# A written-out order for a gated recurrence and its MLP: all words re-ordered, h's casts spread over three engines, the verdicts summed in a row

## The chip, the cores and the metric

The kernel runs on one core of a Trainium2 chip. The metric is device time in microseconds (us) of one execution, the median over the runs shown; lower is better. The engines are TensorE (PE in the rows; PEld is its weight load), VectorE (DVE), ScalarE (ACT), GpSimd (POOL) and SyncE (SP), which here issues nearly all DMA transfers. Each engine works through its own queue in order, and an instruction waits at the head of its queue until what it reads is written and what it overwrites is free.

## What is computed

Inputs q, k, v and alpha have 4 batches, 8 heads, 768 time steps and 48 channels. Each head runs a gated recurrence, and the result goes through a gated MLP of 384 to 1536 to 384 on 3072 tokens:

```python
for t in range(S):
    state = alpha[:, :, t, :, None] * state + np.einsum('bhd,bhe->bhde', k[:, :, t], v[:, :, t])
    y[:, :, t] = np.einsum('bhd,bhde->bhe', q[:, :, t], state)
...
g = x @ w_gate
silu = g * (1.0 / (1.0 + np.exp(-g)))
val = x @ w_val
return (silu * val @ w_out).astype(np.float32)
```

The weights and inputs arrive as the reference has them, the weights in 64 bits.

## The kernel before

**Units.** Time is cut into 16 units (4 per batch, 192 steps of three chunks of 64). A unit u is loaded (words La, Lk, Lq, V), its alpha, k and q are turned so that channels lie on partitions (by TensorE for units 0 to 3: the words p, T, ea, ek, cq; by VectorE's 32x32 transposes for the others: tr, tk, tq, line 399), and VectorE runs two scans over them: G backward (line 472), f forward (lines 478 to 482). The word mk puts k into the first scan's result, q multiplies q by the second's, and qc copies its odd heads. K and kc (units 0 to 3) or kr (line 540, the other units) lay k out in rows. TensorE then forms scores (S, line 565), which VectorE masks (ma, line 606), carries the state over the chunks (C, or the carry at line 584; ad and de bring it into V) and forms outputs (Y, lines 658 to 680). From unit 4 on one word Z, a burst (line 682), holds the outputs of unit u - 1, the scores of unit u and its carry.

**From units to blocks.** The outputs are split into a high and a low part in a 32-bit format that TensorE takes in one pass (yh on ScalarE, line 705; yl on VectorE, line 709) and are regrouped to x, 384 tokens by 384 channels, in blocks of two units: with TensorE and copies for units 0 and 1 (R, line 731, and x, line 735), with SP's transfers for the others (xr, line 745).

**Steps.** The MLP of 8 blocks by 12 slices of 128 hidden channels gives 96 steps s: g (gate product, line 760), sl (SiLU to h, ScalarE, line 768), v (value product, line 760), h (h times v, VectorE, line 772), hh (h cast to the one-pass format, line 776), hl (the rest h - hh, line 781), o (out product, line 793). Each of g, v and o is nine matmuls of 384 columns, as hi and lo parts are multiplied hi by hi, hi by lo and lo by hi. The g and v products have one PSUM bank each (gps, vps), and h, hh and hl have two buffers each, so a step holds up the next one when its h is late. Bursts borrow these banks too (the digits behind @ are banks). Finished rows are copied out (ot, line 805) and stored (os, line 819; those listed in HALVED, line 785, in two halves). The first two blocks run in two halves of the hidden channels, with partial sums spilled to DRAM and added again (pl, line 801).

**Weights.** Twenty groups wl0 to wl19, the first three of one slice piece, the others of two, are loaded and cut from 64 bits to 32 in three steps w.v0, w.v1, w.v2 (lines 163 to 178; if v0 is on ScalarE the other two take another form on VectorE), then split into a high part (w.a, line 343) and a low part (w.p, line 347). Group 3 holds v1 and o0, group 7 holds g4 and v4.

**Checks and the verdict.** Weights and alpha are loaded a second time and checked for range by ScalarE (wr and wc, Lc and ck). VectorE folds the results to one number per partition (fl, line 830), TensorE adds the 128 numbers with a matmul against ones (cp, `counted`, line 841), VectorE converts the sum to an integer flag (fg, line 970), and every engine reads it at the end to decide on a fallback (line 1133).

**The order.** Nothing decides the order at run time. The string ORDER (from line 44) is a list of words `engine:name`, with t, v, s, g, y for TensorE, VectorE, ScalarE, GpSimd and SP; the loop at line 978 issues them one by one, so the words of one letter, read in sequence, are that engine's queue:

```python
for word in ORDER.split():
    e, name = word.split(":")
    name, *banks = name.split("@")
    todo.pop(name)(engines[e], *(BANKS[int(x)] for x in "".join(banks)))
```

## Time and profile before

| | us |
|---|---|
| runs (three) | 548.59, 548.66, 551.18 |
| median | 548.66 |
| profiled execution: its own time | 549.81 |
| profiled execution: its span | 548.1 |
| TensorE busy in the span | 528.0 |
| VectorE busy in the span | 400.5 |

The span runs from the first to the last instruction of the profiled execution; its own time has the launch around it. Busy time counts instructions at work, not waits, register work or DMA issues. An engine's row can have a wait in square brackets, in us, and what ended it. In the rows, `x9` counts instructions that are merged into one row, and a duration in a merged row is that of the whole group.

### The profile page before, as it was taken

The numbers are of one execution on the slowest core, as the hardware profiler recorded it, in microseconds if no ns is written. First come the engines' busy times: TensorE is split into PE (matmuls) and PEld (weight loads), VectorE is DVE, ScalarE is ACT, GpSimd is POOL, SyncE is SP. The second block draws the span as 40 slices with busy tenths as digits, with TensorE's granted clock in tenths as the row PEclk, the third lists the DMA queues.
The fourth block names the chain that finished last, engine by engine and source line by source line (L and its number), as shares of the span: only waits on it lengthen the run. The fifth ranks groups of instructions, "written<-read, shape, count | busy, mean of one in ns | idle before, by whom it ended". The sixth has DMA issues, their size and how long they took to land.

```text
span 548.1 us, 13557 instructions
## 1 busy us (share of the span) xinstructions
PE 528.0 (96%) x5350; PEld 513.7 (94%) x5350; DVE 400.5 (73%) x755; ACT 249.4 (45%) x578; POOL 151.2 (28%) x149
## 2 busy tenths in 40 slices
...
GB/s 243 256 263 292 146 173 249 107 139 174 85 187 151 141 106 185 157 120 73 169 76 101 203 158 112 76 136 129 184 153 73 90 50 158 135 58 104 155 50 47
...
## 3 DMA queue, kind: packets, MB, share of 16 engines
...
## 4 chain that ended last, share of the span: by engine, by line
PE 66%; DVE 3%; DMA 2%; SPq 1%; issue 1%; ACT 0%; POOL 0%; DVEq 0%; POOLq 0%
PE v L760 20%; PE ops L793 20%; PE g L760 20%; PE c L680 2%; PE s L565 1%; DMA L<-in_q_dram 1%; PE c L584 1%; PE y L658 1%; PE y L659 1%; DMA xT<-X 1%; SPq L745 1%; DMA V<-in_v_dram 1%; DVE h L772 0%; DVE V L629 0%; DVE K L540 0%
## 5 line engine op out<-in xcount | busy, mean ns | idle before, releaser
L760 PE MATMUL v<-xT,w 128*128 128x384 f32 x864 | 167.3, 337 | 0.6 <-DMA xT<-X 0.6
L760 PE MATMUL g<-xT,w 128*128 128x384 f32 x864 | 166.6, 336 | 0.6 <-ACT h L768 0.4
L793 PE MATMUL ops<-w,hh 128*128 128x384 f32 x576 | 158.5, 336 | 0.0
L760 PEld LDWEIGHTS v<-xT,w 128*128 128x128 f32 x864 | 150.5, 188 | 2.2 <-issue 0.9
L760 PEld LDWEIGHTS g<-xT,w 128*128 128x128 f32 x864 | 150.7, 188 | 1.8 <-ACT h L768 0.9
L781 POOL TENSOR_TENSOR hl<-h,hh 128x384 fp32r<-128x384 f32 x65 | 69.8, 1075 | 285.5 <-ACT hh L776 271.8
L772 DVE TENSOR_TENSOR h<-h,v 128x384 f32<-128x384 f32 x96 | 53.0, 552 | 89.9 <-PE v L760 61.6
L793 PEld LDWEIGHTS ops<-w,hh 128*128 128x128 f32 x576 | 105.5, 188 | 0.3
L768 ACT ACTIVATE h<-g 128x384 f32<-128x384 f32 x96 | 47.1, 490 | 119.6 <-PE g L760 101.0
L776 ACT CAST hh<-h 128x384 fp32r<-128x384 f32 x96 | 49.1, 511 | 112.0 <-DVE h L772 77.4
L793 PE MATMUL ops<-w,hl 128*128 128x384 f32 x288 | 96.8, 336 | 0.0
L540 DVE STREAM_TRANSPOSE K<-Gs 32x192 f32<-32x192 f32 x192 | 71.1, 370 | 3.3
L793 PEld LDWEIGHTS ops<-w,hl 128*128 128x128 f32 x288 | 54.0, 188 | 0.0
L347 POOL TENSOR_TENSOR w<-t,w 128x768 fp32r<-128x768 f32 (+1 forms) x15 | 27.5, 1842 | 34.4 <-ACT w L343 25.3
L781 DVE TENSOR_TENSOR hl<-h,hh 128x384 fp32r<-128x384 f32 x31 | 18.4, 594 | 22.8 <-ACT hh L776 22.7
L481 DVE TENSOR_TENSOR_SCAN AT<-AT,back 128x771 f32<-128x771 f32 x16 | 29.2, 1824 | 0.6
L606 DVE TENSOR_TENSOR X<-s,mask 64x384 f32<-64x384 f32 (+1 forms) x48 | 26.3, 551 | 3.8 <-PE s L565 3.1
L472 DVE TENSOR_TENSOR_SCAN Gs<-AT,inj 128x772 f32<-128x772 f32 x16 | 28.5, 1780 | 0.5 <-ACT AT L866 0.3
L497 POOL TENSOR_TENSOR X<-trq,AT 112x768 f32<-112x768 f32 x11 | 18.7, 1703 | 32.1 <-DMA xT<-X 11.0
L320 ACT ACTIVATE wc<-wc,wbias 128x384 f32<-128x384 f32 x36 | 23.3, 648 | 1.2
...
L893 POOL TENSOR_TENSOR Gs<-trk,Gs 128x768 f32<-128x768 f32 x9 | 15.3, 1700 | 26.0 <-DVE Gs L472 22.2
...
## 6 DMA issues: line engine op xcount, KB each, us to landing
...
```

Source lines behind the costliest of these rows:

```text
L320: nc.scalar.activation(dev, dev, AF.Relu, bias=wbias, scale=-1.0, accum_out=wviol[:, 0, i : i + 1])
L347: eng.tensor_tensor(out=lo, in0=src, in1=hi.bitcast(F32), op=ALU.subtract)
L472: nc.vector.tensor_tensor_scan(*(x.rearrange("p g t -> p (g t)")[:, ::-1] for x in (Gs, AT, inj)), 0.0, op0=ALU.mult, op1=ALU.add)
L481: nc.vector.tensor_tensor_scan(Af, Af, back[:, 1 : n + 1], back[:, 0:1], op0=ALU.mult, op1=ALU.add)
L540: nc.vector.transpose(out=bass.AP(k0.tensor, k0.offset, [k0.ap[0], (G * 2 * D, NU), (2 * D, GF), (1, 32)]), in_=Kg[j * BO + x : j * BO + x ...
L606: nc.vector.tensor_tensor(out=X[r, z, f * GF : (f + 1) * GF, :].rearrange("r g (c t) -> r g c t", c=NU), in0=sps[f][r].rearrange("r g (c t ...
L760: nc.tensor.matmul(pt, wsp[kind, f][a][:, kt * P : (kt + 1) * P], xT[blk][:, b_, kt, :], start=(n == 0), stop=(n == 3 * KT - 1),)
L768: nc.scalar.activation(h, acc.pop(("g", blk, f)), AF.Silu)
L772: nc.vector.tensor_tensor(out=h, in0=h, in1=acc.pop(("v", blk, f)), op=ALU.mult)
L776: nc.scalar.copy(out=hh, in_=acc["h", blk, f])
L781: eng.tensor_tensor(out=hl, in0=acc.pop(("h", blk, f)), in1=hh.bitcast(F32), op=ALU.subtract)
L793: nc.tensor.matmul(ops[blk][i], h[b_][:, i * P : (i + 1) * P], wsp["o", f][a], start=(first and n == 0), stop=(last and n == 2),)
```

## The change

The order is another one throughout: all five queues are dealt anew. It holds the same words but for two (cp goes, vr comes), and 113 words stand under another engine's letter, among them 44 of the 96 hh, all of which were ScalarE's: 22 now stand under VectorE and 22 under GpSimd. Of hl 18 move from GpSimd to VectorE and 13 the other way; the remaining 38 are cuts and splits of the weights, copies (qc, ot, pa, pq, vc, x) and products (mk, q) that change between VectorE, ScalarE and GpSimd. In place of the matmul against ones, the word vr sends the 128 numbers by a transfer of SP into one row of the identity matrix's tile, and VectorE sums that row and converts the sum. One store is no longer halved.

The code:

```diff
-    def hidden_hi(blk, f):
+    def hidden_hi(blk, f, eng):
         hh = acc["hh", blk, f] = p2.tile([P, NB], F32R, tag="hh", name=f"hh{blk}_{f}", bufs=NH)
-        nc.scalar.copy(out=hh, in_=acc["h", blk, f])
+        (eng.copy if eng is nc.scalar else eng.tensor_copy)(out=hh, in_=acc["h", blk, f])
...
-    HALVED = ((6, 0), (6, 1), (6, 2))
+    HALVED = ((6, 0), (6, 1))
...
-    ones = cp.tile([P, 1], F32, name="ones")
...
-        nc.vector.memset(ones, 1.0)
...
-    def counted(bank):
-        oks.append(ps.tile([1, 1], F32, tag=bank, name="cps"))
-        nc.tensor.matmul(oks[-1], ones, oks[-2], start=True, stop=True)
+    row = ident[0:1, 0:P]
+
+    def verdict_row(eng):
+        eng.dma_start(out=row.rearrange("o (p x) -> o p x", x=1), in_=oks[-1])
+
+    def counted():
+        total = cp.tile([1, 1], F32, name="total")
+        nc.vector.tensor_reduce(total, row, axis=AX.X, op=ALU.add)
+        nc.vector.tensor_copy(out=flag, in_=total)
...
-    todo["cp"] = lambda eng, bank: counted(bank)
-    todo["fg"] = lambda eng: eng.tensor_copy(out=flag, in_=oks[-1])
+    todo["vr"] = lambda eng: verdict_row(eng)
+    todo["fg"] = lambda eng: counted()
```

The order, old (-) and new (+), up to the first products:

```diff
-s:first y:La0 s:pa0 t:Ta0@23 s:ea0 y:wl0 y:Lq0 s:pq0 v:w0v0 v:w0v1 v:w0v2 v:G0 v:f0 t:Tq0@03 v:q0 y:La1 s:pa1 t:Ta1@72
-s:w0a v:w0p y:Lk1 s:pk1 y:Lk0 s:pk0 y:wl1 s:w1v0 t:Tk1@14 y:Lq1 t:Tk0@05 g:pq1 y:V0.2 y:V0.3 y:V0.1 v:w1v1 v:mk0 s:ea1
-v:G1 s:ek1 v:mk1 s:qc0 t:K0.2@0 s:kc0.2 t:K0.1@7 s:kc0.1 t:K0.0@2 s:kc0.0 t:S0@05 t:Tq1@71 s:cq1 v:f1 g:q1 g:qc1
-y:V0.4 y:wl3 y:V0.0 y:V0.5 t:C0.0@2 s:ad0.0 t:K1.1@4 t:K1.0@1 t:C0.1@7 y:wl2 y:V1.1 y:V1.4 y:La2 s:w3v0 s:ad0.1
-s:kc1.0 v:ma0.1 v:ma0.0 v:ma0.2 v:w2v0 v:pa2 v:w2v1 v:w1v2 v:w3v1 s:vc0 t:C0.2@2 s:ad0.2 t:K1.2@7 s:kc1.2 s:kc1.1
-t:Y0@36 s:yh0.0 y:La3 t:Ta2@20 s:pa3 s:ea2 y:Lk2 y:V1.0 s:w1a s:yh0.1 g:w1p y:Lq2 y:V1.3 y:V1.5 y:V1.2 v:w3v2 v:de1
-t:S1@71 t:C1.0@2 s:ad1.0 v:yl0.0 v:ma1.2 t:Ta3@15 t:C1.1@4 s:ad1.1 t:C1.2@0 y:wl4 s:w4v0 s:ad1.2 g:pq2 g:pk2 g:vc1
-v:ma1.1 v:yl0.1 v:ma1.0 t:Y1@64 s:yh1.0 v:w2v2 v:w2a s:yh1.1 t:R0.1@0 t:R0.2@3 t:Tq2@72 s:x0.2 s:x0.1 s:cq2 v:G2
-v:yl1.0 v:yl1.1 t:R1.1@6 s:x1.1 v:w4v1 v:w4v2 t:Tk2@74 v:mk2 v:f2 v:q2 y:Lk3 s:pk3 t:R1.0@0 t:R0.0@6 y:V2.4 s:x0.0
-s:x1.0 t:R1.2@7 s:x1.2 t:K2.0@2 s:kc2.0 g:w2p y:wl5 s:w5v0 y:V2.2 y:V2.0 y:Lq3 g:pq3 s:w4a t:Tk3@34 t:K2.1@7 s:kc2.1
-t:g0 s:sl0 y:V3.1 y:V2.1 y:wl7 y:V2.3 y:V2.5 v:de2 g:vc2 g:lm0 y:V3.2 y:wl8 y:wl6 y:V3.3 y:V3.0 v:w5v1 s:ea3 v:G3
...
+s:first y:La0 s:pa0 t:Ta0@23 s:ea0 y:wl0 y:Lq0 s:pq0 t:Tq0@03 v:w0v0 v:w0v1 v:w0v2 v:G0 v:f0 v:q0 s:w0a v:w0p y:La1
+s:pa1 t:Ta1@15 y:Lk1 s:pk1 y:Lk0 s:pk0 y:wl1 s:w1v0 t:Tk1@26 v:w1v1 t:Tk0@47 v:mk0 s:ea1 s:ek1 v:G1 y:wl2 s:w2v0 v:mk1
+y:Lq1 s:pq1 y:V1.4 t:K0.2@6 t:K0.0@2 t:K0.1@1 s:kc0.2 y:V0.4 s:kc0.0 s:kc0.1 v:w1v2 y:V0.2 y:V0.0 y:V0.1 t:S0@43
+t:Tq1@27 s:cq1 v:f1 g:q1 g:qc1 y:wl3 v:w3v0 v:ma0.2 y:V0.3 y:V0.5 t:C0.0@0 s:ad0.0 t:K1.0@6 s:kc1.0 v:qc0 v:ma0.1
+t:C0.1@5 s:ad0.1 v:ma0.0 t:K1.1@7 s:kc1.1 y:La2 y:V1.0 t:C0.2@6 s:vc0 s:ad0.2 t:K1.2@2 s:kc1.2 s:w1a s:pa2 t:S1@07
+t:Y0@16 s:yh0.0 y:V1.1 y:V1.5 y:wl4 y:V1.3 y:V1.2 v:de1 t:C1.0@3 v:w2v1 v:w2v2 v:w3v1 v:w3v2 s:ad1.0 t:Ta2@45 s:ea2
+s:yh0.1 t:C1.1@3 s:ad1.1 s:w3a y:Lq2 y:La3 v:ma1.2 t:C1.2@5 v:ma1.0 v:ma1.1 g:vc1 t:Y1@24 v:yl0.1 v:yl0.0 s:ad1.2
+s:pa3 t:R0.2@6 t:R0.1@7 t:Ta3@53 g:pq2 y:V2.3 y:V2.4 y:Lk2 y:Lk3 y:V2.5 g:w1p g:pk2 v:G2 s:w4v0 v:w4v1 v:x0.1 s:x0.2
+s:yh1.0 v:yl1.0 s:yh1.1 t:Tq2@60 s:cq2 s:w2a g:w3p v:yl1.1 t:Tk2@71 v:mk2 t:R0.0@2 s:pk3 s:x0.0 t:R1.0@6 s:x1.0
+t:R1.2@7 t:R1.1@4 s:x1.1 s:x1.2 t:K2.0@2 s:kc2.0 t:g0 s:sl0 y:wl15 y:V3.0 y:V2.2 y:V2.1 y:V3.3 y:V2.0 v:de2 t:C2.0@2
+s:vc2 v:w2p v:f2 v:q2 y:wl10 y:V3.2 y:V3.1 y:Lq3 s:ea3 t:Tk3@41 t:g1 t:K2.1@7 v:w4v2 s:ad2.0 v:G3 s:w4a g:w4p v:mk3
...
```

Around the new order's steps 2 and 3, the burst of unit 10, the first product of block 5, and the end:

```diff
+y:xr2.2 y:wl12 y:V4.0 v:hl1 t:o0 t:o1 t:g3 v:w7v0 v:ma3.2 v:ma3.1 t:Y3@12 v:w7v1 y:La4 s:w8v0 v:w7v2 v:w8v1 v:h2 s:w7a
+v:w7p v:lm1 y:Lk4 v:w8v2 v:w9v1 s:hh2 v:w9v2 v:hl2 s:sl3 s:w11v0 s:yh3.0 s:yh3.1 s:w8a t:g4 t:v3 v:w8p v:h3 s:w9a t:o2
...
+v:G11 v:ma9.2 v:ad9.2 v:tk11 t:v44 g:mk11 v:h44 t:g43 s:sl43 t:v43 v:tq11 v:h43 v:hh43 v:hl43 t:g45 s:sl45 y:V10.5
+y:V10.2 y:V10.3 y:V10.4 v:kr10.3 t:Z10@02165 s:yh9.0 s:yh9.2 s:wc15 v:yl9.0 v:ma10.2 v:ma10.1 y:V11.2 y:V11.1 y:V11.3
...
+v:hl55 y:xr11.0 t:o55 s:yh11.1 v:ma12.2 v:yl11.1 y:xr11.1 s:yh11.2 v:yl11.2 y:xr11.2 v:ma12.0 v:kr13.2 v:tq13 t:o56
+t:v57 v:h57 g:hh57 g:hl57 t:g58 v:ma12.1 v:f13 g:q13 s:ad12.0 s:sl58 t:v58 v:h58 t:g60 s:sl60 t:v60 v:kr13.1 v:h60
...
-s:hh93 g:hl94 g:hl93 t:v95 t:g95 s:sl95 t:o93 t:o94 v:h95 s:hh95 v:hl95 t:o95 t:cp@2 v:ot95.0 y:os95.0 v:ot95.1
-s:ot95.2 y:os95.1 s:oz0 y:oz1 v:fg
...
+s:sl92 t:v92 t:o90 v:h92 s:hh92 v:fl y:vr v:hl92 t:o91 t:o92 t:g93 s:sl93 t:v93 v:h93 v:hh93 s:hh94 v:hl94 v:hl93
+t:g95 s:sl95 t:v95 t:o93 t:o94 v:h95 s:hh95 v:hl95 t:o95 v:fg v:ot95.0 y:os95.0 v:ot95.1 s:ot95.2 y:os95.1 s:oz0 y:oz1
```

## Rows read from the trace of the kernel before

**Rows 1.** The head of the page: the span, and TensorE's busy time, share and instructions.

```profile
span 548.1 us, 13557 instructions
...
PE 528.0 (96%) x5350; PEld 513.7 (94%) x5350; DVE 400.5 (73%) x755; ACT 249.4 (45%) x578; POOL 151.2 (28%) x149
```

**Rows 2.** Busy time by stretches: from:to, length, then each engine's busy us.

```profile
0.00:20.00 20.00, 10.86 (x137) 9.24 (x137) 16.97 (x27) 13.89 (x29) 11.88 (x29) 1.00 0.89 250
20.00:40.00 20.00, 18.18 (x388) 15.30 (x388) 19.34 (x31) 18.04 (x44) 8.88 (x12) 1.00 0.88 251
...
160.00:180.00 20.00, 19.72 (x114) 19.43 (x113) 18.68 (x41) 5.61 (x13) 10.25 (x8) 1.00 0.65 159
...
480.00:500.00 20.00, 20.00 (x117) 20.00 (x116) 4.27 (x8) 9.76 (x26) 2.54 (x3) 1.00 0.31 91
```

In these rows the engines are TensorE, its weight load, VectorE, ScalarE and GpSimd, each with its count of instructions; behind them stand the granted clock, the share of the DMA engines and GB/s.

**Rows 3.** TensorE's waits: line, waited for, total us, times, longest.

```profile
PE y L658 <- DVE h L772: 1.8, 1, 1.8
...
PE c L584 <- issue: 1.0, 1, 1.0
PE v L760 <- DMA xT<-X: 0.6, 1, 0.6
```

**Rows 4.** The timeline of the start: start us, us, engine, line, operation.

```profile
31.26 1.02 DVE L709 TENSOR_TENSOR Y<-y,Y 112x384 fp32r<-112x384 f32 x2
...
33.51 0.95 PE L731 MATMUL xp<-Y,sel 112*128 112x384 f32 x4
...
35.54 0.82 PE L419 MATMUL pt<-ident,wide 128*128 128x128 f32 x6
...
36.51 1.84 PE L760 MATMUL g<-xT,w 128*128 128x384 f32 x9
```

**Rows 5.** VectorE's groups by line and shape: busy us, mean ns of one.

```profile
L164 DVE SCALAR_TENSOR_TENSOR t<-raw,t 128x768 uint32<-128x768 uint32 x14 | 13.3, 952 | 0.1
...
L805 DVE COPY ot<-ops 128x384 f32<-128x384 f32 x9 | 4.9, 554 | 4.0 <-ACT hh L776 2.0 <-PE ops L793 1.9
...
L172 DVE TENSOR_SCALAR t<-raw 128x768 uint32<-128x768 uint32 x2 | 2.0, 1018 | 0.0
L178 DVE SCALAR_TENSOR_TENSOR t<-raw,t 128x384 uint32<-128x384 uint32 x2 | 2.0, 976 | 0.1
...
L407 DVE COPY wide<-L 128x576 f32<-128x576 f32 x1 | 0.8, 761 | 0.0
L172 DVE TENSOR_SCALAR t<-raw 128x384 uint32<-128x384 uint32 x2 | 0.7, 355 | 1.2 <-DMA raw<-in_moe_w_gate_dram 1.2
...
L343 DVE CAST w<-t 128x384 fp32r<-128x384 f32 x1 | 0.5, 473 | 0.0
```

**Rows 6.** hh by line (mean ns), and hl on two engines: shortest/median/longest ns.

```profile
L776 ACT CAST hh<-h 128x384 fp32r<-128x384 f32 x96 | 49.1, 511 | 112.0 <-DVE h L772 77.4 <-PE ops L793 34.4
...
L781 POOL TENSOR_TENSOR hl<-h,hh x65: 1004/1018/2137, 47.8 to 536.6; 128x384 fp32r<-128x384 f32 x65
L781 DVE TENSOR_TENSOR hl<-h,hh x31: 525/558/1377, 51.3 to 540.5; 128x384 fp32r<-128x384 f32 x31
```

**Rows 7.** The timeline at step 2: its value product and its h.

```profile
52.72 1.85 PE L760 MATMUL v<-xT,w 128*128 128x384 f32 x9
...
56.12 0.53 DVE L772 TENSOR_TENSOR h<-h,v 128x384 f32<-128x384 f32 x1
```

**Rows 8.** The timeline before the burst of unit 10.

```profile
263.73 1.65 DVE L399 STREAM_TRANSPOSE AT<-L 128x768 f32<-128x768 f32 x1
...
269.27 1.52 DVE L540 STREAM_TRANSPOSE K<-Gs 32x192 f32<-32x192 f32 x4
...
274.02 1.61 DVE L399 STREAM_TRANSPOSE trq<-L 128x768 f32<-128x768 f32 x1 [2.02 <-DMA L<-in_q_dram]
...
278.74 0.55 DVE L772 TENSOR_TENSOR h<-h,v 128x384 f32<-128x384 f32 x1
...
279.34 0.27 PE L658 MATMUL y<-X,V 128*64 128x64 f32 x1 [1.76 <-DVE h L772]
```

More of the change, by code (lines that the diff above doesn't have):

```diff
@@ L55 @@
-t:g0 s:sl0 y:V3.1 y:V2.1 y:wl7 y:V2.3 y:V2.5 v:de2 g:vc2 g:lm0 y:V3.2 y:wl8 y:wl6 y:V3.3 y:V3.0 v:w5v1 s:ea3 v:G3
-t:S2@20 s:qc2 v:ma2.2 v:mk3 v:ma2.0 v:lm1 y:wl11 y:wl9 y:V3.4 y:V3.5 s:w3a g:w3p g:w4p v:ma2.1 t:C2.0@7 t:K2.2@1
-s:kc2.2 s:ad2.0 t:g1 t:v0 t:C2.1@3 v:h0 s:ad2.1 s:sl1 t:K3.0@7 s:kc3.0 t:Tq3@03 t:C2.2@1 s:ad2.2 s:cq3 s:hh0 s:w6v0
-v:f3 t:v1 t:K3.1@7 t:g2 v:w5v2 g:hl0 v:h1 v:q3 v:de3 v:w6v1 s:hh1 s:kc3.1 s:sl2 t:Y2@20 s:yh2.0 v:hl1 v:w6v2 t:C3.0@4
-t:S3@67 s:w5a g:w5p t:v2 s:ad3.0 t:C3.1@1 s:yh2.1 v:ma3.2 v:w8v0 v:yl2.0 s:w6a g:w6p t:o0 t:o1 v:ma3.1 v:yl2.1 y:wl12
@@ L60 @@
-y:La4 y:V4.5 y:wl10 s:w7v0 s:qc3 v:h2 v:ma3.0 y:xr2.0 y:xr2.1 v:w7v1 v:w7v2 v:w8v1 s:w9v0 s:ad3.1 s:vc3 t:g3 v:w8v2
-v:w9v1 y:Lk4 y:wl13 y:xr2.2 t:Y3@20 s:sl3 s:w7a s:hh2 v:hl2 v:w7p s:w8a v:w8p s:yh3.0 s:yh3.1 t:v3 v:h3 s:w10v0 v:w9v2
-s:hh3 v:hl3 t:g4 v:w10v1 s:sl4 s:w9a g:w9p t:o2 t:v4 v:yl3.1 v:yl3.0 v:h4 s:hh4 g:hl4 t:g5 v:w10v2 v:w10a s:w11v0
-s:sl5 s:w12v0 t:v5 t:o3 v:w11v1 v:w10p t:g6 s:sl6 v:w12v1 v:w11v2 s:w11a v:h5 g:w11p s:hh5 t:o4 g:hl5 v:w12v2 y:xr3.0
-y:xr3.1 y:xr3.2 y:wl16 y:V4.1 y:wl14 t:v6 v:tk4 v:h6 s:hh6 g:hl6 t:g7 v:tr4 v:G4 s:sl7 s:w13v0 s:w12a y:Lq4 v:mk4
```

160 lines of the change are left out of this document (81 added, 79 removed).

## The prediction

> **What bounds the kernel now.** I read the head of the page first: TensorE is busy for 528.0 us of a span of 548.1 [rows 1]. The reader should see that TensorE's work, not its waiting, is the time: 20.1 us of the span is all that any order can win, and a part of it cannot go (the first load before the first transpose, the last store after the last product). The time by stretches comes next [rows 2]: TensorE is short of 20 us by 9.1 in the first 20 us and by 1.8 in the second; later stretches are full or nearly so. VectorE is as full as TensorE up to 180 us (19.34 and 18.68 of 20) and nearly idle at the end (4.27). So the kernel has two halves: up to some 200 us two engines run side by side with no air, and the order decides which waits; after that VectorE has room, and TensorE waits only where one buffer or one load is late. The list of TensorE's waits names those [rows 3]: 1.8 us in front of a burst for a VectorE product, 1.0 us inside a burst that the profile puts down to nothing, 0.6 us for rows of x. With a few smaller ones they are all that is lost after 40 us: 3.4 us in these three.
>
> **The change, part by part.** The list of TensorE's pieces is the same, less the last count; what is new is their order, that of the other queues, and 113 instructions that change engine. I price it against the profiled execution, 549.81 us with a span of 548.1; the median of the runs shown is 1.15 us lower, and at the end I take that off.
>
> *The start.* The first product g0 waits for x of units 0 and 1, which waits for VectorE's yl1.1. In the old order that ended at 32.28 us (31.26 + 1.02) [rows 4]. Counting the words up to yl1.1 in both orders, VectorE gains w3v0 (1.02), w4v1 (0.95), and two copies, qc0 and x0.1 (0.55 each), and gives up w2v0 (0.36), pa2 (0.76) and w2a (0.47); w2's third cut goes from the 0.98 form to one that I price as the copies, 0.55 [rows 5]. That is +1.06, so 33.3. Four repacks follow on TensorE (0.95 for two [rows 4], so 1.9): 35.2. ScalarE then copies x1.1 and x1.2 (0.51 each, as its cast of this shape [rows 6]): 36.3. The last third of g0 comes after that (a third of 1.84 [rows 4]), so g0 ends at about 36.9; it ended at 38.35 before. But the old order had put Tk3 and K2.1 ahead of g0, 0.97 us from 35.54 to 36.51 [rows 4], and the new one has them behind it: 36.9 + 0.97 = 37.9, or 0.5 sooner. ScalarE speaks for later: its queue up to x1.2 takes five instructions more (w2v0, pq1, pa2, w3a, w2a) and three less (qc0, w3v0, x0.1), at 0.5 to 1.0 us each between -0.5 and +3.5, and it had 2.0 us of air in 20 to 40 us [rows 2], so up to +1.5 can show. **I take 0.0**, nearer to VectorE's count, which is the one with the rows, and keep -1.0 and +1.5 as bounds.
>
> *From g1 to g5.* Up to g2, and again up to g5, both orders hold the same TensorE pieces, so what counts is whether VectorE keeps up. Up to h2 it has 7.6 us more (w3v0 and w7v0 at 1.02; w7v1, w7v2, w8v1 at 0.95; hl0, ma3.0, w2p and the two copies at 0.55) and 4.0 less (w2v0, pa2, w2a and the shorter cut as above, q3 at 0.95, w8v0 at 1.02), all at the price of the nearest shape in [rows 5]: +3.6. h2 ended 2.1 us after its product v2 [rows 7]; it would end 5.7 after it. Nothing needs it before v3 and o2, and between v2 and o2 stand five groups of nine (117 matmuls in 20 us [rows 2], so 1.55 each, 7.75) and the outputs of unit 3. Then w7p, three cuts and hl2 follow (5.7 + 4 x 0.95 + 0.55 = 10.0), which uses the room up: 0.0, with the upper end in the rivals.
>
> *h converted elsewhere.* 44 of the 96 casts hh leave ScalarE (511 ns each [rows 6]): 22 go to VectorE, 22 to GpSimd. ScalarE is busy for 5.6 of 20 us in mid-run [rows 2], so its relief buys nothing. On VectorE a cast of this shape took 0.47 [rows 5]. On GpSimd no cast of it is in the trace; between 0.47 and the 2.14 of its longest subtraction, I take 1.02, the median of hl on that engine and shape [rows 6]. What hides it is the room between a step's last product and its out product: among the GpSimd steps at least three groups (4.65, step 83), against h 0.55 [rows 8], hh 1.02 and hl 1.02, 2.6 in all; among the VectorE steps two groups (3.1), against at most 0.55 + 0.47 + 1.02. So 0.0; at the upper price step 83 needs 4.8 and would wait 0.2. VectorE's subtraction took 525 to 1377 ns and GpSimd's 1004 to 2137 [rows 6]: medians sit near the shortest, with a tail as long as one of each, one after the other. [...]
>
> *The burst of unit 10.* It needs the bank of the last v product, so the last h before it. That h stood behind tq11, which waited 2.02 us for a load that VectorE's tr11 releases: 265.38 to 274.02, then to 279.29, and TensorE lost 1.76 [rows 8]. In the new order ten groups again lie between v41 and the burst. Behind tq11 only h43 is left: 1.61 + 0.55 in place of 5.27, so 3.1 earlier. But before h41 VectorE has one kr group more (1.52) and TensorE one group less (1.55), and it had 0.3 us of air there: 2.8 later. Net **-0.3**; bounds -1.76 and +1.4 (if the load still ends as late and h41 is late on top).
>
> *x of unit 11.* The 0.6 us wait stood in the first product of block 5, for the last rows of x [rows 3]. In the new queue of SP no store and no V load stand between those rows' transfers, and VectorE's scan f13 no longer splits their yl. TensorE comes one group (1.55) sooner. Bounds -0.6 and +1.0; I take **-0.6**.
>
> *The verdict.* The count on TensorE goes (it ran beside the last copies). SP sends the row (vr) behind fl; behind it on SP stand only the last stores. fg waits for it on VectorE, ahead of ot95.0 and ot95.1. Eight groups lie between (12.4 us), and even the slow load of [rows 8] took 8.6. 0.0; without that cover the last store would wait by the rest. One store that is no longer halved saves an issue that nobody waits for.
>
> *Sum:* 549.8 - 0.3 - 0.6 = 548.9 on the profiled scale, **547.8** on that of the median. The 1.0 us inside a burst I leave, for I see no cause that the order touches.
>
> **Rivals.** *All waits go, and the start comes early.* If g0 is 1.0 us sooner and all three waits of [rows 3] vanish (3.4), 4.4 are won: 544.3. For it: these waits are accidents of one order. Against it: VectorE stays full up to 180 us [rows 2], and every burst is re-dealt, so new accidents are as likely. 0.26.
>
> *VectorE becomes the bound around v3.* g4 needs w7p, which now stands right behind h2: 5.7 + 0.95 = 6.6 us after v2, against three groups (4.65) and unit 3's outputs; o2 needs hl2 behind four cuts. From the point where VectorE loses another 0.5 us in the first 50 us, TensorE pays one for one, and nothing later gives it back, since both are full. Price: up to 2.0 there (6.6 - 4.65), and 1.5 from ScalarE's longer queue, with the old waits kept: 549.8 + 3.5, 552.2 on the median's scale. For it: +3.6 us ahead of h2; against it: VectorE is relieved again by h5. 0.18.
>
> *It only permutes.* The casts leave an engine that bounds nothing, and the waits move elsewhere: 548.7. That lies in my forecast's own case.
>
> **The numbers.** The forecast's case, 546 to 550, has 0.56. The range reaches from 543.9 to 551.8, close to the middle of either rival, which leaves out about half of each. Half a per cent is 2.7 us, about what a measurement of this kernel can tell from no change. Faster by more is the first rival: 0.26; slower by more the second: 0.18; within it 0.56.
>
> **What would show it.** g0 should end near 37 us with Tk3 behind it, and g5 near 69.7. TensorE's wait for a VectorE h in front of burst 10 should shrink, not go; that for xT in block 5 should be gone. GpSimd's hh should read near 1.0 us, with no TensorE wait for hl. The end should keep its 5 us. I am wrong if TensorE's busy time itself changes, if the first 70 us differ by more than 1.5, or if a new wait of over 1 us stands in mid-run.

## The result, and the profile after

The new order was slower: **554.94 us** (median of four runs, 553.96 to 556.14) against 548.96 before (four runs, 548.59 to 551.18), a ratio of **1.0101** [1.0066, 1.0137]. The forecast was 547.8, and its range ended at 551.8. The profiled execution of the new kernel took 553.96, its span 552.2; the old one's took 549.81, with a span of 548.1. That pair differs by 4.15 us and the medians by 5.98: the profiled execution is the fastest of the new kernel's four, at a mean granted clock of 0.999, and the other three, at 0.995 and 0.996, took 0.4 to 2.2 us longer. What follows accounts for the pair.

The head of the page after, with the queue that brings TensorE's instructions:

```profile
span 552.2 us, 13582 instructions
...
PE 528.7 (96%) x5348; PEld 514.8 (93%) x5348; DVE 410.6 (74%) x779; ACT 233.7 (42%) x542; POOL 159.9 (29%) x161
...
q8 instruction: 43, 0.70, 0.6%
```

TensorE's work is what it was: 528.7 busy against 528.0 [rows 1]. The 4.1 us of span are waits. The moved casts show in ScalarE (249.4 to 233.7), VectorE (400.5 to 410.6) and GpSimd (151.2 to 159.9).

The stretches that answer to [rows 2]:

```profile
0.00:20.00 20.00, 11.66 (x138) 10.08 (x138) 16.86 (x27) 14.16 (x31) 10.66 (x28) 1.00 0.87 237
20.00:40.00 20.00, 17.44 (x340) 15.40 (x339) 19.37 (x31) 17.50 (x43) 8.57 (x8) 1.00 0.81 228
40.00:60.00 20.00, 18.17 (x310) 16.41 (x309) 18.97 (x27) 16.72 (x38) 10.14 (x8) 1.00 0.74 224
160.00:180.00 20.00, 20.00 (x116) 20.00 (x116) 18.13 (x37) 5.80 (x14) 8.44 (x6) 1.00 0.78 192
```

From 160 us on, the waits are too short for this scale and have to be sought one by one. TensorE's list of waits after (compare [rows 3]):

```profile
PE c L583 <- issue: 2.5, 1, 2.5
PE s L564 <- issue: 1.8, 1, 1.8
...
PE c L583 <- DMA V<-in_v_dram: 1.0, 1, 1.0
...
PE v L759 <- DVE h L771: 0.9, 2, 0.5
PE s L564 <- POOL X L496: 0.7, 1, 0.7
PE ops L792 <- ACT ot L804: 0.4, 1, 0.4
```

Two of [rows 3] are gone, as forecast: the product before a burst (1.8) and x of unit 11 (0.6). But the wait that the profile puts down to nothing ("issue") has grown from 1.0 to 2.5, and a second one of 1.8 has come. Their places, in TensorE's timeline after:

```profile
51.11 0.87 PE L564 MATMUL s<-X,Gs 48*64 48x64 f32 x43
53.81 0.34 PE L564 MATMUL s<-X,Gs 48*64 48x64 f32 x5 [1.83 <-issue]
...
395.32 0.89 PE L564 MATMUL s<-X,Gs 48*64 48x64 f32 x48
396.02 0.47 PE L583 MATMUL c<-V,K 64*48 64x48 f32 x20
398.97 0.56 PE L583 MATMUL c<-V,K 64*48 64x48 f32 x28 [2.48 <-issue]
```

The first stands inside the scores of unit 3 (S3), the second inside the carry of burst 14 (Z14). Each breaks a run of identical small matmuls off in the middle, and the profile shows nothing that either waits for.

How far the new order is behind the old one, at points where TensorE has done the same set of pieces (after minus before, from the two timelines):

| up to | behind, us | what came or went |
|---|---|---|
| x of units 0 and 1 | 0.10 | |
| S3 and C3.0 | 1.85 | S3's stall, 1.83 |
| g10 | 1.70 | |
| g22 | 3.35 | h late at v14, v15, g16 (0.99 in three); Z6 waits 1.01 for a V load, where before lost 0.36 at g22 |
| v30 | 3.56 | |
| Z10 | 2.07 | the wait of 1.76 before burst 10 is gone |
| block 5's first products | 1.6 | the wait for x of unit 11 (0.57) is gone |
| before Z14 | 2.62 | among it the wait for ScalarE's copy ot at o60, 0.4 |
| behind Z14 | 4.08 | the stall is 2.48 where it was 1.02 |
| end of the span | 4.1 | |

So in this pair of profiles 3.3 of the 4.1 us stand at two stalls without a named releaser: 1.83, and 2.48 - 1.02 = 1.46. (The section on the first 65 us shows that the runs without S3's stall won 0.2 us of the 1.8 or less, as VectorE was late there too.) The casts, of which the change is named, read:

```profile
L775 ACT CAST hh<-h 128x384 fp32r<-128x384 f32 x52 | 26.6, 512 | 79.7 <-DVE h L771 49.7 <-PE ops L792 29.5 <-PE y L658 0.5
L775 POOL CAST hh<-h 128x384 fp32r<-128x384 f32 x22 | 11.2, 508 | 106.3 <-DVE h L771 38.2 <-PE ops L792 30.4 <-DVE hl L780 12.5
L775 DVE CAST hh<-h 128x384 fp32r<-128x384 f32 x22 | 8.7, 398 | 2.6 <-PE ops L792 1.4 <-issue 0.4
L780 POOL TENSOR_TENSOR hl<-h,hh 128x384 fp32r<-128x384 f32 x60 | 69.9, 1166 | 165.9 <-ACT hh L775 106.1 <-DVE hh L775 43.5 <-PE ops L792 7.6
```

### The profile page after: what moved, and what is told of

Same layout as the page of the kernel before. It is cut to its first block, busy times and chain, and to the rows that moved or that the text cites. A ratio compares the mean times of both kernels' runs of the same rounds, so it can differ in the third digit from the quotient of the medians.

```text
span 552.2 us, 13582 instructions
## 1 busy us (share of the span) xinstructions
PE 528.7 (96%) x5348; PEld 514.8 (93%) x5348; DVE 410.6 (74%) x779; ACT 233.7 (42%) x542; POOL 159.9 (29%) x161
## 4 chain that ended last, share of the span: by engine, by line
PE 79%; DVE 10%; DMA 3%; issue 3%; SPq 2%; ACT 1%; POOL 0%; DVEq 0%; ACTq 0%; POOLq 0%
PE ops L792 24%; PE v L759 24%; PE g L759 23%; DVE K L539 2%; PE s L564 2%; PE c L679 1%; PE pt L418 1%; SPq L442 1%; DVE AT L480 1%; DVE X L605 1%; PE y L657 1%; DMA L<-in_k_dram 1%; DMA Le<-in_q_dram 1%; PE y L658 1%; PE c L583 1%
## 5 line engine op out<-in xcount | busy, mean ns | idle before, releaser
L759 PE MATMUL v<-xT,w 128*128 128x384 f32 x864 | 167.1, 337 | 1.3 <-DVE h L771 0.9
L759 PE MATMUL g<-xT,w 128*128 128x384 f32 x864 | 166.6, 336 | 0.4 <-ACT h L767 0.3
L759 PEld LDWEIGHTS v<-xT,w 128*128 128x128 f32 x864 | 150.7, 188 | 3.3 <-DVE h L771 2.2
L759 PEld LDWEIGHTS g<-xT,w 128*128 128x128 f32 x864 | 151.0, 188 | 1.1 <-ACT h L767 0.6
L780 POOL TENSOR_TENSOR hl<-h,hh 128x384 fp32r<-128x384 f32 x60 | 69.9, 1166 | 165.9 <-ACT hh L775 106.1
L775 ACT CAST hh<-h 128x384 fp32r<-128x384 f32 x52 | 26.6, 512 | 79.7 <-DVE h L771 49.7
L775 POOL CAST hh<-h 128x384 fp32r<-128x384 f32 x22 | 11.2, 508 | 106.3 <-DVE h L771 38.2
L496 POOL TENSOR_TENSOR X<-trq,AT 112x768 f32<-112x768 f32 x12 | 20.8, 1730 | 36.9 <-DMA xT<-X 11.1
L780 DVE TENSOR_TENSOR hl<-h,hh 128x384 fp32r<-128x384 f32 x36 | 19.8, 556 | 10.6 <-POOL hh L775 7.7
```

The source lines that it names most:

```text
L759: nc.tensor.matmul(pt, wsp[kind, f][a][:, kt * P : (kt + 1) * P], xT[blk][:, b_, kt, :], start=(n == 0), stop=(n == 3 * KT - 1),)
L775: (eng.copy if eng is nc.scalar else eng.tensor_copy)(out=hh, in_=acc["h", blk, f])
L780: eng.tensor_tensor(out=hl, in0=acc.pop(("h", blk, f)), in1=hh.bitcast(F32), op=ALU.subtract)
```

## What the "issue" stalls are

*Theory A.* TensorE is waiting for its own instructions. Queue q8 brought 0.70 MB in 43 packets, 16 KB each, and TensorE's trace holds some 10,800 instructions: about 256 to a packet. Counted in trace order, S3's stalled instruction is number 1473 = 5 x 256 + 193, and Z14's number 8641 = 33 x 256 + 193, the latter in both kernels. Every stall of this kind inside a burst, in every run below, stands at a multiple of 256 plus 193. The packet is in each case just ahead: at S3 it ran from 51.36 to 52.47 and TensorE resumed at 53.81; at Z14 from 396.41 to 397.54, resuming at 398.97; before, from 392.54 to 393.49, resuming at 394.89. Some 1.3 to 1.5 us lie between landing and resuming. Z14 is 168 matmuls with their weight loads in about 3 us, so it uses up a block in 2.3 us without a stall (measured in e12, below) and meets two block edges. In stretches of 384-column products, 117 matmuls in 20 us [rows 2] and as many weight loads, a block lasts some 22 us, and the list of waits shows none at such an edge. So much for what the count and the packets show; that the fetch causes the stall has to be tested.

*Theory B.* The fetch is late because it shares the DMA engines with data. *Theory C, the rival:* the stall belongs to the burst itself (its operands or banks) and would stay wherever the edges lie.

Experiments shift the edges with idle instructions, which the word `al` puts in:

```diff
     for word in ORDER.split():
         e, name = word.split(":")
         name, *banks = name.split("@")
+        if name.startswith("al"):
+            nc.tensor.addr_align(256, int(name[2:]))
+            continue
```

**e1.** 96 and 81 idle instructions in the new order, each in one lump, so that Z14 meets another edge, and back again behind Z15.

```diff
-t:g65
+t:al238 t:g65
...
-t:v76
+t:al46 t:v76
```

> The changed kernel with idle instructions put into TensorE's queue, no other edit: some 96 ahead of group g65, so that burst Z14 begins 72 instructions into a 256-instruction block instead of 232, and some 81 ahead of v76, so that burst Z15 begins at 100 and holds one block edge as before. Theory A (TensorE runs out of instructions: Z14 holds two block edges, and the second block is not there in time): the 2.48 us stall inside Z14 goes, 554.9 - 2.5 = 552.4, if the idle instructions cost nothing beside the long matmuls. Theory B (the stall is a wait for data or for a bank that the profile does not name): the stall stays, 554.9 or more.

562.73, ratio 1.0272 [1.0208, 1.0336]. Z14's stall is gone; the lumps themselves became waits. TensorE's timeline at the first lump, and the stretches on either side of its end:

```profile
389.63 2.69 PE L759 MATMUL g<-xT,w 128*128 128x384 f32 x8 [3.81 <-issue]
```

```profile
386.00:389.60 3.60, 0.00 (x0) 0.00 (x0) 3.43 (x8) 1.79 (x6) 0.00 (x0) 1.00 0.48 108
389.60:394.00 4.40, 4.37 (x16) 4.39 (x17) 3.99 (x9) 0.49 (x1) 0.00 (x0) 0.61 0.92 244
```

After 3.81 us idle the granted clock is 0.61 in this stretch, and eight matmuls take 2.69 us, where the nine of the product ahead of the lump took 1.73. This lump cost its own time and then some.

**e2, e3, e4.** One lump behind Z14 only (a control); the same as e1 in the old order; and 120 and 136 around S3.

```diff
-t:o74
+t:al203 t:o74
```

> The changed kernel with some 96 idle instructions in TensorE's queue between Z14 and Z15, ahead of o74: a control for the one ahead of Z14. Theory A: Z14's stall stays at 1 to 2.5 us, since the place of its block edges is the same, and Z15, which then begins 19 instructions into a block, has its one edge at its 237th instruction, some 2 us after its start: 554.9, or up to 1 us more. Theory B, in the form that idle instructions of themselves end such a stall: as the kernel with the pads ahead of Z14. If idle instructions cost time on their own, it shows here: 96 of them, above 554.9.

561.17, 1.021 [1.0167, 1.0253]. With the edges ahead of it unmoved, Z14 still stalled for 1.14 and S3 for 2.12; TensorE's waits:

```profile
PE ops L792 <- issue: 4.5, 1, 4.5
...
PE s L564 <- issue: 2.1, 1, 2.1
PE c L583 <- issue: 1.1, 1, 1.1
```

e3, in the old order:

```diff
-t:g64
+t:al220 t:g64
...
-t:g76
+t:al45 t:g76
```

> The kernel before with the same kind of idle instructions ahead of its Z14 (which begins 231 instructions into a block there) and of its Z15. Theory A: its one stall of this kind, 1.02 us inside Z14, goes: 1.0 us faster than the kernel before, 547.9. Theory B: no change, 548.9.

563.85, 1.0257 [1.0195, 1.0318]; Z14's stall is gone here too, the lumps cost 8.8 in two, and S3, which had no stall in the old kernel's profile, shows one of 1.1 (0.57 and 0.65 in two later runs of that order, e9 and e15).

```diff
-t:v1
+t:al57 t:v1
...
-t:g4
+t:al38 t:g4
```

> The changed kernel with some 120 idle instructions ahead of v1, so that the pair of bursts Y2 and S3 has its block edge 112 instructions after its start instead of 232 and the block before it 6.6 us long instead of 4.4, and some 136 ahead of g4, which put all later work back to its old place in the blocks. Theory A: the 1.83 us stall inside S3 goes: 554.9 - 1.8 = 553.1; the pads stand in a stretch where TensorE's queue is short, so up to 2 us of them could show instead. Theory B: the stall stays, 554.9 or more.

574.15, 1.044 [1.0393, 1.0487]. S3's stall went, Z14's stayed at 1.4, and 120 idle instructions cost 8.6 us, 72 ns each. Theory C falls with these four: the same bursts with the same operands lose the stall when the edges move. The later runs agree. With its edges moved, Z14 ran through in six profiles of six (e1, e3, e5, e6, e10, e11) and S3 in four of four (e4, e8, e10, e16). With its edges unmoved, S3 of the new order stalled in seven of seven (0.71 to 2.12), and Z14 of either order in eleven of twelve; the twelfth is e12, below. The times say nothing of the stall's worth, as the lumps cost more than it.

**e5, e6.** The shift spread out: eight idle instructions ahead of each of ten products before Z14 and of ten before Z15. At 72 ns each (e4) eight are 0.58 us, beside products of 1.55 us.

```diff
-t:g64
+t:al42 t:g64
...
-t:g66
+t:al20 t:g66
...
-t:v76
+t:al29 t:v76
```

> The changed kernel with the same shift as in the run with pads ahead of Z14, but with the idle instructions spread: 8 ahead of each of ten groups before Z14 (which then begins 56 instructions into a block) and of ten before Z15 (which begins at 83). One took 71 ns in the queue, so 8 take 0.57 us beside a group of 1.55 us, and TensorE should not see them. Theory A (instructions come too late): Z14's stall (2.48, 1.14 in two profiles) goes at no price, 554.9 - 1.8 = 553.1, between 552.4 and 554. Theory B (idle instructions ended the stall by the pause that they made, not by the place of the block edge): the stall stays, 554.9.

In e6, in the old order:

```diff
-t:v62
+t:al23 t:v62
...
-t:g65
+t:al1 t:g65
...
-t:g76
+t:al15 t:g76
```

> The kernel before with 8 idle instructions ahead of each of ten groups before Z14 and of ten before Z15. Theory A: its stall in Z14 (1.02 us) goes, 1.0 us faster than the kernel before on this chip (ratio 0.998). Theory B: ratio 1.000.

e5: 552.2, ratio 1.0077 [1.005, 1.0103], against 1.0101 [1.0066, 1.0137] for the unshifted order; the intervals overlap, so the gain in time is not shown. In its profile Z14 runs through, and ends 2.24 us earlier than in the new kernel:

```profile
54.14 2.90 PE L759 MATMUL v<-xT,w 128*128 128x384 f32 x9
...
395.86 0.89 PE L564 MATMUL s<-X,Gs 48*64 48x64 f32 x48
396.56 0.73 PE L583 MATMUL c<-V,K 64*48 64x48 f32 x48
```

The first row shows why the time gained less than that: S3 stalled for 1.43 and the clock fell after it, so that v2 took 2.90 us; it had taken 1.84 in the new kernel after its stall of 1.83. The stretch from 54 to 58 us of e5:

```profile
54.00:58.00 4.00, 4.00 (x36) 3.42 (x31) 3.92 (x7) 3.33 (x7) 2.40 (x2) 0.57 0.32 74
```

e6: 548.54, ratio 1.0039 [0.9998, 1.0079], inconclusive: its profiled run took 547.1 with Z14's stall gone, the others up to 552.45.

**e12.** Theory B: two loads for checks (wr13, Lc14) and the checks themselves moved from in front of Z14 to behind it. No idle instructions, so the edges stay.

```diff
-y:wr13 y:os59.2 y:Lc14 y:La15
+y:os59.2 y:La15
...
-t:Z14@10625 s:wc13 s:hh65
+t:Z14@10625 s:hh65
...
-t:o65 s:ck14 s:wc10
+t:o65 s:wc10
...
-y:V15.6 y:Lc3
+y:V15.6 y:wr13 y:Lc14 y:Lc3
...
-s:yh13.2 s:ck3
+s:yh13.2 s:wc13 s:ck14 s:ck3
```

> The changed kernel with two loads of 384 and 288 KB (wr13 and Lc14) and the work on them moved from right ahead of Z14 to behind it; no idle instructions, so Z14's block edges stay where they are. The 16 KB block that Z14 waits for was asked for while these loads were under way and began 2.31 us after TensorE entered the block before it. If the block waits behind other transfers, the stall in Z14 (2.48, 1.14, 1.44, 1.69 and 0.99 us in five profiles of this order) shrinks to 0.5 to 1.0 us; if the transfers have nothing to do with it, it stays in 1.0 to 2.5 us.

554.65, 1.0107 [1.0079, 1.0135], so no better in time, but Z14's stall vanished. In the new kernel, the stretch from TensorE's entry into the block to the start of the fetch of the next:

```profile
394.10:396.40 2.30, 2.30 (x136) 2.19 (x131) 1.06 (x3) 1.75 (x4) 1.04 (x2) 1.00 0.73 140
```

In e12 the corresponding stretch:

```profile
393.10:395.30 2.20, 2.20 (x136) 2.13 (x130) 2.16 (x4) 1.62 (x4) 1.00 (x1) 1.00 0.09 15
```

and the transfers within e12's burst and e12's TensorE at the end of it:

```profile
q1 hardware_dynamic: 200, 0.04, 8.3%
q8 instruction: 1, 0.02, 2.4%
```

```profile
395.00 0.91 PE L583 MATMUL c<-V,K 64*48 64x48 f32 x48
...
408.23 1.83 PE L759 MATMUL g<-xT,w 128*128 128x384 f32 x9 [1.20 <-ACT h L767]
```

With the DMA engines at 0.73, the fetch began 2.31 us after the entry into the block; at 0.09 it began at the entry itself. Every other profile whose Z14 stands at this place in the blocks can be read in the same way. The DMA share is that of the first microsecond after the entry:

| profile | fetch begins, us after the entry | DMA engines | stall, us |
|---|---|---|---|
| new kernel | 2.31 | 0.99 | 2.48 |
| e7 | 1.44 | 0.99 | 1.69 |
| e13 | 1.30 | 1.07 | 1.68 |
| e4 | 1.19 | 0.91 | 1.44 |
| kernel before | 1.07 | 0.63 | 1.02 |
| e2 | 0.93 | 0.96 | 1.14 |
| e8 | 0.56 | 1.10 | 0.99 |
| e14 | 0.56 | 0.62 | 0.49 |
| e9 | 0.37 | 0.38 | 0.33 |
| e16 | 0.16 | 0.91 | 0.33 |
| e15 | at the entry | 0.00 | 0.20 |
| e12 | at the entry | 0.00 | none |

The stall follows the start of the fetch: packet, landing and first use take 2.3 to 2.8 us from there on, about as long as the burst takes for a block, so a late start shows nearly in full. What makes the start late is less sure. With idle DMA engines it was not late (e12, and e15, where Lc14 alone was moved away); with busy ones it was 0.16 to 2.31 late, and their share does not say how late (e16 and the new kernel). So theory B holds for Z14 as far as this: in the two profiles without data transfers at the entry (0.00) the fetch was not late. How late it is with them varies between executions, and for S3, where no run moved loads, the theory is not tested.

Z14 ended 3.62 us earlier than in the new kernel, of which 1.02 had been gained ahead of it; 1.20 went at g68, because the moved checks stood in front of its SiLU on ScalarE. e12's median is no better than the new kernel's, and its executions divide by the mean granted clock: the three at 0.998 to 1.000 took 551.79 to 553.36, the five at 0.989 to 0.993 took 554.05 to 557.28. What lowered the clock in those five is not in the one profile, which is of the fastest execution.

## The first 65 us: a second cause under the first

**e8.** S3's edges moved without idle instructions, by letting v2 and C3.0 go first.

```diff
-t:S3@01
+t:v2 t:C3.0@4 t:S3@01
```

> The changed kernel with group v2 and C3.0 ahead of S3 on TensorE, where they stood right behind it; no idle instructions. This puts 2.1 us more work between the two block edges around Y2 and S3 (4.4 us becomes 6.5), and S3's operands are as ready as before. Theory A: the stall in S3 (1.83, 0.71 and 2.12 us in three profiles) goes, 554.9 - 1.8 = 553.1. Theory B (S3 waits for something in its data that the profile does not name): the stall moves with S3 or stays in time, 554.9. VectorE's product after S3 comes 0.3 us earlier than with the stall.

553.61, 1.0107 [1.0064, 1.0149]: S3's stall went, and nothing was won. e8's list of waits, TensorE's g4, and the VectorE, GpSimd and ScalarE rows:

```profile
PE g L759 <- ACT h L767: 2.3, 2, 2.0
```

```profile
63.42 3.10 PE L759 MATMUL g<-xT,w 128*128 128x384 f32 x9 [2.00 <-ACT h L767]
```

```profile
55.09 2.17 POOL L346 TENSOR_TENSOR w<-t,w 128x768 fp32r<-128x768 f32 x1 [0.90 <-ACT w L342]
...
55.47 2.54 DVE L171 TENSOR_SCALAR t<-raw 128x768 uint32<-128x768 uint32 x1
...
61.70 0.55 DVE L771 TENSOR_TENSOR h<-h,v 128x384 f32<-128x384 f32 x1
...
62.34 0.51 ACT L775 CAST hh<-h 128x384 fp32r<-128x384 f32 x1 [0.55 <-DVE h L771]
62.87 0.49 ACT L767 ACTIVATE h<-g 128x384 f32<-128x384 f32 x1
```

VectorE forms h2 late, ScalarE's cast hh2 waits for it, and behind hh2 in ScalarE's queue stands sl3, which frees the bank that g4 waits for. In the new kernel the same rows on ScalarE are:

```profile
61.93 0.51 ACT L775 CAST hh<-h 128x384 fp32r<-128x384 f32 x1 [0.82 <-DVE h L771]
62.47 0.49 ACT L767 ACTIVATE h<-g 128x384 f32<-128x384 f32 x1
```

There TensorE, already 1.8 late, arrives when sl3 is done; in the old order sl3 stands in front of hh2. So two causes of nearly the same size lie side by side, and taking one away shows the other. In e8 it cost more than the wait of 2.00: after it the granted clock read 0.70 from 62 to 66 us (1.00 in the new kernel), g4 took 3.10 us where it had taken 1.86, and by v3 TensorE was 1.54 behind the new kernel.

Part of h2's lateness is one VectorE instruction. In e8 the cut w7v0 took 2.54 us (0.55 in the new kernel); it began while GpSimd was splitting a weight (w6p) and ended 0.75 after that split. In the new kernel the same happened two cuts later:

```profile
56.27 3.08 POOL L346 TENSOR_TENSOR w<-t,w 128x768 fp32r<-128x768 f32 x1 [2.00 <-ACT w L342]
...
57.67 2.49 DVE L177 SCALAR_TENSOR_TENSOR t<-raw,t 128x768 uint32<-128x768 uint32 x1
```

The cut of 2.49 took 0.96 in e8, and it ended 0.81 after w6p. No run takes w6p away, so that it is what held VectorE up is read from the rows and not tested.

**e10.** Both away, and e5's shift for Z14.

```diff
-t:S3@01
+t:v2 t:C3.0@4 t:S3@01
...
-v:h2 s:w7a
+v:h2 s:sl3 s:w7a
...
-v:hl2 s:sl3
+v:hl2
...
-t:g64
+t:al42 t:g64
...
```

> The changed kernel with three edits: v2 and C3.0 ahead of S3 (no stall in S3), sl3 ahead of w7a and hh2 on ScalarE as the kernel before has it, and the spread idle instructions before Z14 and Z15. Where only v2 and C3.0 were moved, TensorE waited 2.0 us for sl3 ahead of g4, since sl3 stood behind hh2, which waits for VectorE's late h2. If that chain is the second cause in the first 65 us, both go now: 1.8 us there and 1.8 in Z14, 554.9 - 3.6 = 551.3, and g5 ends near 69.7 us instead of 71.5. If VectorE itself is behind there (v3's bank waits for h2, o2 for hl2), the wait moves to v3 or o2 and 553 is left.

551.69 (ten runs), ratio **1.004** [1.0008, 1.0072]. Both stalls and the 2 us at g4 are gone from the trace. The ratio fell by 0.0061, 3.3 us, with intervals that just touch. The profile puts this gain at Z14: there TensorE goes from 0.77 us behind the new kernel to 2.01 ahead. The first 65 us won next to nothing. This execution's start was 1.30 late (granted clock 0.57 from 14 to 22 us); taking that off, TensorE was 1.85 ahead of the new kernel behind S3, and 0.23 at o2. The difference went in waits for VectorE, with the time around them: 0.52 for hl1, whose subtraction took 2.25 us beside w6p, and 0.28 at g4 for w7p. In e16 (next section), with the same two edits, g4 waits twice:

```profile
62.13 0.62 PE L759 MATMUL g<-xT,w 128*128 128x384 f32 x2 [0.42 <-ACT w L342]
63.47 1.51 PE L759 MATMUL g<-xT,w 128*128 128x384 f32 x7 [0.72 <-DVE w L346]
```

There g5 ends at 71.53, in the new kernel at 71.55. So the other outcome that the expectation names came true: VectorE itself is behind there, and S3's stall lies on top of it. How far is open, since the edit has a share in it: it puts S3 later, and VectorE then waited 0.79 to 0.91 us for S3's scores (e8, e10, e16), against 0.42 in the new kernel. e8's expectation had them 0.3 earlier. (In e1, where S3 stalled for 0.71 and no VectorE instruction took over 1.6 us in that stretch, g5 ended at 70.75, and the shorter stall was a gain in full.) What is left of the loss in e10, 0.4%, is not settled: this lateness of VectorE, the ledger's late h, Z6's load and o60 are in it.

## The other parts, one by one

**e9.** The casts, the verdict row and the unhalved store alone, in the old order.

```diff
-s:hh9 t:g11
+v:hh9 t:g11
...
-s:hh93 g:hl94 g:hl93
+y:vr v:hh93 g:hl94 g:hl93
...
-t:o95 t:cp@2 v:ot95.0
+t:o95 v:fg v:ot95.0
```

> The kernel before, its order of all queues kept word for word, with the changed kernel's other parts: the 44 casts hh of the change on VectorE and GpSimd, the verdicts summed in a row by VectorE, one store no longer halved. My theory (the time went with the order, the parts are free): 1.000 of the kernel before, between 0.997 and 1.003. Rival (the casts on VectorE and GpSimd make h late and TensorE waits for hl): up to 1.007, with waits of TensorE for hl in the trace.

562.67, 1.0246 [1.0207, 1.0285]: the parts, put into the old order, are far from free, and the waits in the trace are those of the casts. TensorE's waits in e9, and the longest on GpSimd:

```profile
PE ops L793 <- POOL hl L781: 2.8, 2, 2.1
PE s L565 <- ACT h L768: 2.0, 1, 2.0
```

```profile
489.76 0.51 POOL L776 CAST hh<-h 128x384 fp32r<-128x384 f32 x1 [4.84 <-DVE h L772]
490.23 1.95 POOL L781 TENSOR_TENSOR hl<-h,hh 128x384 fp32r<-128x384 f32 x2
```

GpSimd's cast hh83 waits 4.84 us for its h, hl82 stands behind it, and o82 waits 2.13 us for hl82. It is not the cast's 0.51 us that costs, but whom it keeps waiting.

**e13.** The reverse: all 44 hh back on ScalarE in the new order.

```diff
-v:h10 v:hh9
+v:h10 s:hh9
...
-v:h20 g:hh20
+v:h20 s:hh20
...
```

> The changed kernel with one part undone: all 44 moved casts hh back on ScalarE, each at its place in the new order; nothing else. In the old order the same 44 moves cost 14 us. If the new order has made them free (my first reading, casts beside other work), this is 554.9, within 1.5 us either way. If they cost time in the new order too, this is faster, 553 or less. If the new order leans on them (its queues are arranged so that ScalarE is free), it is slower, 557 or more.

562.15, 1.0228 [1.017, 1.0286], worse again, with SiLUs late behind the casts (PE g L759 waits 3.0 us in three for ACT's h). The casts' new engines and the new order lean on each other: either alone is slower than both together, and both together are slower than neither.

**e7, e16.** The V load that Z6 waits for. e7 takes its issues ahead of the transfers xr4; e16 does the same, moves La7 behind it too, and has e10's first two edits.

```diff
-y:xr4.0
+y:V6.0 y:V6.1 y:V6.4 y:V6.5 y:xr4.0
...
-s:sl20 y:V6.0 y:V6.1 y:os18.2 y:V6.4 y:V6.5 v:tq6
+s:sl20 y:os18.2 v:tq6
```

and in e16 besides

```diff
-y:V6.7 y:La7 y:pl18.1
+y:V6.7 y:pl18.1
...
-s:sl20 y:os18.2
+s:sl20 y:La7 y:os18.2
```

> The changed kernel with the last four loads of V of unit 6 moved in SP's queue from behind the ten xT transfers and two stores to ahead of them. The last of them landed at 158.75 us, when Z6's last stretch went on after 1.0 us of waiting. All theories agree on that wait: it goes, 1.0 us, 553.9. If V of unit 6 is not what Z6 waited for, or if the xT transfers, 2.6 us later, are missed by block 2, 554.9 or more.

> The changed kernel with v2 and C3.0 ahead of S3 and sl3 ahead of hh2 as before, and in SP's queue the four loads of V of unit 6 and the xT transfers ahead of the four loads La7 (3.0 us of issue), so that neither V nor the transfer that frees q6's buffer is late for Z6. No idle instructions. The 1.0 us wait in Z6 goes and no other takes its place (moving the V loads alone turned it into a 2.3 us wait for q6): 1.0 us there and 1.0 to 1.8 in the first 65 us, 552.5. If La7 comes too late for tr7 on VectorE, which is full there, up to 1.5 of it is given back.

e7: 555.72, 1.0131 [1.0106, 1.0157]. The wait for V became one for GpSimd's q6, since xr4 came later:

```profile
158.56 1.68 POOL L496 TENSOR_TENSOR X<-trq,AT 112x768 f32<-112x768 f32 x1 [4.18 <-DMA xT<-X]
```

e16: 553.96, 1.0115 [1.0053, 1.0176]. Z6's wait went, o19 waits 1.19 for a partial sum instead. Both are misses: in SP's queue each load that went ahead made another late.

**e14, e15, e11.** The waits that the change removed, removed from the old order: tq11, f11 and Lk12 behind h44 (e14), with Lc14 behind Z14 as well (e15).

```diff
-v:tq11
...
-y:Lk12
...
-v:f11 v:h44 v:kr10.1 t:Z10@12506
+v:h44 v:kr10.1 v:tq11 v:f11 y:Lk12 t:Z10@12506
```

and in e15 besides

```diff
-t:Z14@21506 y:Lc14
+t:Z14@21506
...
-s:yh13.1 s:ck14
+s:yh13.1
...
-v:hl66 y:wr14
+v:hl66 y:Lc14 y:wr14
...
-s:wc10
+s:wc10 s:ck14
```

> The kernel before with tq11, f11 and the load Lk12 behind h44 and kr10.1, just ahead of Z10, so that h44 waits for no load. TensorE's wait ahead of Z10 (1.76, 1.16, 1.01 and 0.97 us in four profiles of this order) goes: 1.0 to 1.7 us faster than the kernel before, ratio 0.997 to 0.998. If what stood behind h44 is now late (yl9.0, ma10.2 behind 3.4 us of tq11 and f11), ratio 1.000 with a wait of TensorE inside Z10 or behind it.

> As the run with h44 ahead, and the 288 KB load Lc14 with its check ck14 moved behind Z14, so that less is under way when Z14's second block of instructions is fetched. Z14's stall (1.02 us in the profile of before, 0.33 in that with the moved casts) goes or shrinks to 0.3 us: a further 0.5 us, ratio 0.996 to 0.997. If the block does not wait behind that load, the same as without it.

e14: 551.27, 1.0045 [1.0015, 1.0074]; e15: 552.01, 1.0049 [1.002, 1.0079]. Z10's wait is gone in both, and v45 waits 1.8 us for VectorE's yl9.0, which now stands behind tq11 and f11. Neither ratio need be the price of the edit: in both profiles 2.7 to 2.9 us were lost by the end of g0, far ahead of the first edited word, with the granted clock at 0.57 from 14 to 18 us (1.00 in the old kernel's profile). From g0 to the end e14's profile is 0.7 us faster than the old kernel's and e15's 2.5 slower. So the record does not show that the edit costs anything, only that it won nothing that the runs can tell. Z14's stall reads 0.20 in e15, but also 0.49 in e14 and 0.33 in e9 with Lc14 in its place, so its size adds little for theory B; what e15 adds is the start of the fetch, at the entry, with the DMA engines idle:

```profile
396.80:398.00 1.20, 1.20 (x67) 1.13 (x66) 1.08 (x3) 1.17 (x4) 0.45 (x1) 1.00 0.00 0
```

e11, in the old order, put h44 ahead of tq11 and f11 but kept Lk12 early, with e6's shift:

```diff
-v:tq11 v:ad9.2
+v:ad9.2
...
-v:f11 v:h44 v:kr10.1
+v:h44 v:tq11 v:f11 v:kr10.1
```

> The kernel before with the spread idle instructions before its Z14 and Z15, and with tq11 and f11 behind h44 on VectorE, so that h44 no longer waits behind a load. Theory A for Z14: no stall there (1.0 us in the profile of before). The wait ahead of Z10 (1.76, 1.16 and 1.01 us in three profiles) should go too. Together 2.0 us faster than the kernel before, ratio 0.996; if only one of the two goes, 0.998.

In e11 Lk12's load lands in the tile that tq11 still has to read, so unit 11 is computed from other numbers, and tq11 waits for that load. 549.58, 1.0016 [0.9992, 1.004]: no gain; Z10's wait came back as 1.54 for kr10.1. No version here was measurably faster than the old kernel.

## Why the prediction was wrong

- **The step that failed first in the sum** was "The 1.0 us inside a burst I leave, for I see no cause that the order touches." It was one of the three waits that the prediction took from [rows 3], and I put its change at nothing. It is the fetch of TensorE's next block: the stall went when the burst began elsewhere in a block (e1, e5), and the fetch began 2.31 us late beside loads and not late in e12, where two of them had been moved away. In the pair of profiles it went from 1.02 to 2.48, 1.46 of the 4.1 us. Part of that is the luck of two executions: over all profiles with this edge and these loads the stall was 0.33 to 2.48 in the new order (mean 1.4, seven profiles) and 0.33 to 1.02 in the old (mean 0.6, three).
- **From g1 to g5 (0.0)**, "Nothing needs it before v3 and o2", failed next: g5 was forecast near 69.7 and ended at 71.55. In the new kernel's trace S3's stall of 1.83 stands there, a second wait of the same kind that the prediction did not look for. But in the runs without that stall (e8, e10, e16) waits for VectorE, and for what hangs on it, took at least 1.6 of it back. I counted who reads h2, and not who stands behind its reader: hh2 on ScalarE, in front of sl3, which g4 needs; that cost 2.00 in e8, and more by the clock after it. And h2 was later than counted. It seems right, 5.44 us after its product (61.84 - 56.40) where 5.7 was forecast, but only because S3's stall had held the product back. Against the old kernel h2 came 5.2 later (56.65 to 61.84), where the count of VectorE's work said 3.6; 1.5 of the difference is the one cut of 2.49. The second rival had the place, the sign and the price (2.0 there), and its way, by w7p, shows in e16. Its total of 552.2 was 2.7 short; it held 1.5 for ScalarE's queue that did not come, and nothing for Z14.
- **The start** (0.0): right. g0 ended at 37.34, forecast 36.9, and the ledger stands at +0.10 behind the repacks.
- **Casts** (0.0): right as to this order, and for the wrong reason. GpSimd's hh took 508 ns where I had taken 1.02 us, VectorE's 398 where I had taken 0.47, hl on GpSimd 1166 ns on average (1075 before), with no TensorE wait for hl. But "its relief buys nothing" does not hold in the new order: e13, which takes the relief back, loses 7 us against the new kernel. And that the casts cost nothing does not hold in the old one: e9 loses 14. The room between product and out product was counted in groups; what decides is the queue order on the receiving engine.
- **Burst 10** (-0.3; bounds -1.76 and +1.4): the wait of [rows 8] went altogether, so the term was at its lower bound, not at the value taken. **x of unit 11** (-0.6): right, -0.57. **The verdict** (0.0): right; some 5 us lie between TensorE's end (547.0) and the span's, as before.
- **New waits in mid-run** (v14 to g16, Z6, o60) were named only as a sign of error; they cost 2.4 us (0.99 + 1.01 + 0.4), about what the two removed ones gave (1.76 + 0.57). "It only permutes" described the rest, but not the first 65 us and Z14.
